# A delta-rule attention with a GELU block on one core: V of chunk 1 scaled between the query masks, exponents moved forward on ScalarE

## The chip, the cores and the metric

The kernel runs on one core of a Trainium2 chip. The metric is device time in microseconds for one execution. Four runs of the kernel before took 670.16 to 671.1 us, with a median of 670.89 us.

The engines are TensorE (PE in the profile; its weight loads are PEld), VectorE (DVE), ScalarE (ACT) and GpSimd (POOL). SyncE (SP) issues the loads. Each engine works its own instructions strictly in the order of its queue and waits on semaphores for the others.

## What is computed

The first part is a delta rule: for each of 4 x 8 heads a 48 x 48 state is carried over 768 steps. Its outputs, put side by side for the 8 heads, are 3072 rows of 384 numbers, which go through a two-layer block with an exact GELU.

```python
k_n = k / (np.linalg.norm(k, axis=-1, keepdims=True) + 1e-06)
for t in range(S):
    y[:, :, t] = einsum('bhd,bhde->bhe', q[:, :, t], state)
    v_old = einsum('bhde,bhd->bhe', state, k_n[:, :, t])
    state = state + beta_t * einsum('bhd,bhe->bhde', k_n[:, :, t], v[:, :, t] - v_old)
x = y.transpose(0, 2, 1, 3).reshape(B * S, H * D)
h = x @ w_in                      # 384 -> 2048
out = (0.5 * h * (1 + erf(h / sqrt(2)))) @ w_out
```

Shapes: q, k, v are 4 x 8 x 768 x 48, beta is 4 x 8 x 768, w_in is 384 x 2048, w_out is 2048 x 384. Both weights come in as 64-bit floats and are decoded to 32 bits on the chip.

## The kernel before

**Chunks and units.** The 768 steps are cut into 12 chunks of 64. In a chunk there are two units (`a` = 0, 1), each with two batches on the 128 partitions and all 8 heads. The recurrence inside a chunk is turned into products of K with K (`grams`), of Q with K (`queries`), an inverse of a unit lower triangular matrix by `eliminate_steps`, and per chunk: `against_state` (W from V and the state), `solve` (U = inverse times W, copied from PSUM by eight ScalarE copies, L603), `use` (P times U into PSUM, L615), `update` (the addition to the state, L624, on TensorE), `next_state` (that addition into the state, L629, on VectorE), `read` (four ScalarE copies of the outputs of a unit, L636) and `turn` (transposed outputs xT for the feed-forward part). The feed-forward part of a chunk is sixteen `fc1` groups (L677) with a Gelu each on ScalarE (L679), then the second layer (L690 in the first chunks).

Chunks 0 and 1 are the list `first`: four units, `first[:2]` of chunk 0 and `first[2:]` of chunk 1. Chunk 0 has no state before it, so its W is V times a factor (L562, GpSimd). For chunk 1, V is multiplied by the norms with `scale_v` (L332, GpSimd) before `against_state` of that chunk reads it, at 78.17 us in the profile. `masked` (L405, GpSimd) multiplies the query products P of a unit by a triangular mask, 128 x 512 each; `use` reads P, at 51.6 us for chunk 0 and at 90.2 us for chunk 1.

**Weights.** A weight group of 768 columns is decoded in four steps. `begin(n)` takes the exponent bits (VectorE, L218). `exponents(n)` shifts them (ScalarE, L223). `mantissas(n)` is two VectorE instructions (L228, L230). `signed(n)` is two more (L235, L236), reads the exponents, and asks SP to `fetch` the raw weights of four groups further on, into the same buffer. Groups 0 to 7 are w_in, 8 to 15 are w_out. The raw weights of groups 8 to 10 are fetched early, into buffers that nothing else uses then (`slots`).

**Who sets the order.** There are two parts. Up to `by_hand.close()` the order of all five queues is that of the program text: loads, transposes, `grams`, the elimination of chunk 0 and 1 (VectorE, 18 to 40 us), `back0` to `back2` (the inverse is transposed into XM and Zf; `back2` also clears parts of Zf, once on ScalarE, L464, and three times on GpSimd, L466), two levels of `join`, decoding of groups 0 to 2, and chunk 0. The second level of `join` ends in four ScalarE copies into Zf (L499). After it, VectorE's order is that of a list with due times (`plan`), written out by the program. The order of the other four queues is then set by the framework's planner from its own estimates of when things are ready.

The loads of this part stand on SP in the order of the text; q of chunk 2 and k of chunk 3 go into buffers that become free only when the query transposes have read them.

Of the kernel before, what the change touches and what calls it, by code (L numbers as in the profile page):

```python
# [16 lines left out]
def kernel(  # L17
# [35 lines left out]
    NA = B // 2  # L53
# [15 lines left out]
    def dn(name):  # L69
        return ps.tile([128, 2, 512], F32, tag="dn", name=name)  # L70
# [22 lines left out]
    def fetch_in(dst, src, u, queues=(nc.sync, nc.sync)):  # L93
        rows = slice(u.c * C, (u.c + 1) * C)
        for p in range(2):
            queues[p].dma_start(out=dst[HALF[p]],
                                in_=src[2 * u.a + p, :, rows, :].rearrange("h t d -> t h d"))

    for c in range(NC):
        for a in range(NA):  # L100
            u = tiles[c, a] = Unit()
# [37 lines left out]
    def load_v(c):  # L139
        if c >= NC:  # L140
            return
        for a in range(NA):
            u = tiles[c, a]
            u.V = io.tile([128, H, D], F32, tag="V", name="V", bufs=4)
            fetch_in(u.V, v, u)
# [4 lines left out]
    first = [tiles[c, a] for c in range(2) for a in range(NA)]  # L150
# [48 lines left out]
    def fetch(n):  # L199
        if n >= len(w_parts):  # L200
            return
        dst, src = w_parts[n]
        if n < n_in:
            raw = stage[:, n % NS * 2 * WG:(n % NS + 1) * 2 * WG]
        else:
            raw = slots[(n - n_in) % len(slots)]
        w_raw[n] = raw.rearrange("q (n w) -> q n w", w=2)
        raw = raw.rearrange("q (m n w) -> q m n w", m=dst.shape[1], w=2)
        for m in range(dst.shape[1]):
            nc.sync.dma_start(out=raw[:, m], in_=src[:, m])  # L210
# [3 lines left out]
    def begin(n):  # L214
        e = su.tile([128, WG], U32, tag="w_e", name="w_e")
        raw = w_raw.pop(n)
        halves[n] = w_parts[n][0].rearrange("q m n -> q (m n)"), raw[:, :, 0], raw[:, :, 1], e
        nc.vector.tensor_scalar(e, raw[:, :, 1], 20, 0x7FF, op0=ALU.logical_shift_right,  # L218
                                op1=ALU.bitwise_and)

    def exponents(n):
        e = halves[n][3]
        nc.scalar.activation(e, e, ACT.Relu, bias=lim[:, 0:1], scale=float(2 ** 23))  # L223

    def mantissas(n):
        dst, lo, hi, e = halves[n]
        bits = dst.bitcast(U32)
        nc.vector.tensor_scalar(bits, hi, 0xFFFFF, 0x100000, op0=ALU.bitwise_and,  # L228
                                op1=ALU.bitwise_or)
        nc.vector.scalar_tensor_tensor(dst, lo, 2.0 ** -32, bits, ALU.mult, ALU.add)  # L230

    def signed(n):

        dst, lo, hi, e = halves.pop(n)
        nc.vector.scalar_tensor_tensor(e, hi, 0x80000000, e, ALU.bitwise_and, ALU.bitwise_or)  # L235
        nc.vector.scalar_tensor_tensor(dst, dst, 2.0 ** -20, e.bitcast(F32), ALU.mult, ALU.mult)  # L236
        after = n + (NS if n < n_in else len(slots))
        if (after < n_in) == (n < n_in):
            fetch(after)
# [91 lines left out]
    def scale_v(u, engine=nc.gpsimd):  # L331
        engine.tensor_tensor(u.V, u.V, ns[u.c][:, u.a].unsqueeze(2).to_broadcast([128, H, D]),  # L332
                                op=ALU.mult)
# [70 lines left out]
    def masked(u, engine=nc.gpsimd):  # L404
        engine.tensor_tensor(u.P, u.P, mask_h, op=ALU.mult)  # L405
# [144 lines left out]
    def pairs(ap, s):  # L550

        return ap.rearrange("q (k s r) d -> q k s r d", s=2, r=2)[:, :, s]
# [3 lines left out]
    def against_state(us):  # L556

        for u in us:
            u.W = wk.tile([128, H, D], F32, tag="W", name="W")
            u.y = None  # L560
            if u.c == 0:
                nc.gpsimd.tensor_tensor(u.W, u.V,  # L562
                                        ng[:, u.a].unsqueeze(2).to_broadcast([128, H, D]),
                                        op=ALU.mult)
                continue
            u.psK = dn("psK")[:, :, 0:2 * NP * D].rearrange("q r (x j d) -> q x r j d", x=2, d=D)
            for x in range(2):
                for j in range(NP):
                    for r, p in QUADS:
                        rows = slice(r * C, r * C + D)  # L570
                        to = HALF[p ^ (j % 2)] if x and u.c > 1 else HALF[p]
                        nc.tensor.matmul(u.psK[to, x, r, j, :], lhsT=(u.Qt if x else u.Kt)[rows, p, j, :],  # L572
                                         rhs=St[rows, u.a, p, j, :], start=True, stop=True)
        for u in us:
            if u.c == 0:
                continue
            gm = gms[u.c // 2][:, u.t]
            u.y = wk.tile([128, H, D], F32, tag="y", name="y")
            nc.scalar.copy(heads(u.y), u.psK[:, 1])  # L579
            nc.vector.tensor_tensor(heads(u.W), u.psK[:, 0], heads(u.V), op=ALU.subtract)  # L580
            nc.vector.tensor_tensor(u.W, u.W, gm.unsqueeze(2).to_broadcast([128, H, D]),
                                    op=ALU.mult)

    def quarters(ap):

        return ap.rearrange("q p (k r d) -> q p k r d", r=2, d=D)

    def solve(us, copies=(nc.scalar.copy, nc.scalar.copy)):
        psU = dn("psU")
        for u in us:  # L590
            zf = Zf[(u.c // 2) % 2]
            u.psU = quarters(psU[:, :, u.a * NP * D:(u.a + 1) * NP * D])
            for k in range(NP // 2):
                for r in range(2):
                    for p, s in SIDES:
                        h = 4 * k + 2 * s + r
                        nc.tensor.matmul(u.psU[HALF[p ^ s], p, k, r, :],  # L597
                                         lhsT=zf[HALF[p], u.t * H + h, :],
                                         rhs=u.W[HALF[p], h, :], start=True, stop=True)
        for u, copy in zip(us, copies):  # L600
            u.U = wk.tile([128, H, D], F32, tag="U", name="U")
            for p, s in SIDES:
                copy(pairs(u.U[HALF[p]], s), u.psU[HALF[p ^ s], p])  # L603

    def use(us):

        for u in us:
            psY = dn("psY")
            u.psY = quarters(psY[:, :, 0:NP * D])
            u.psS = psY[:, :, NP * D:2 * NP * D].rearrange("q p (j d) -> q p j d", d=D)  # L610
            for k in range(NP // 2):
                for r in range(2):
                    for p, s in SIDES:
                        h = 4 * k + 2 * s + r
                        nc.tensor.matmul(u.psY[HALF[p ^ s], p, k, r, :], lhsT=u.P[HALF[p], h, :],  # L615
                                         rhs=u.U[HALF[p], h, :], start=True, stop=True)
            if u.c > 0:
                update(u)

    def update(u):  # L620
        if u.c < NC - 1:
            for j in range(NP):
                for r, p in QUADS:
                    nc.tensor.matmul(u.psS[HALF[r], p, j, :], lhsT=u.Kp[HALF[p], 2 * j + r, :],  # L624
                                     rhs=u.U[HALF[p], 2 * j + r, :], start=True, stop=True)
# [5 lines left out]
    def read(u, copy=nc.scalar.copy):  # L631
        u.x = wk.tile([128, H, D], F32, tag="x", name="x")
        for p, s in SIDES:
            dst, src = pairs(u.x[HALF[p]], s), u.psY[HALF[p ^ s], p]
            if u.c < 2:
                copy(dst, src)  # L636
            else:
                nc.vector.tensor_tensor(dst, src, pairs(u.y[HALF[p ^ s]], s), op=ALU.add)  # L638
# [219 lines left out]
        fetch_in(Qp[2 + a][:, :, 0:D], k, tiles[3, a])  # L858
    for n in range(2, NS):
        fetch(n)  # L860
    for n in range(n_in, n_in + len(slots)):
        fetch(n)
    load_v(1)
    third = [tiles[2, a] for a in range(NA)]
    for u in third:
        transposed(u, (0,))
# [9 lines left out]
    nc.vector.scalar_tensor_tensor(ng, gms[0][:, 0:NA], -1.0, ns[0], ALU.mult, ALU.mult)  # L876
    back0[0](*back0[1:])
    against_state(first[:NA])
    for u in first:
        masked(u)  # L880
    back1[0](*back1[1:])
    for a in range(NA):
# [1 line left out]
    back2[0](*back2[1:])  # L884
    for a in range(NA):
        join(0, (a,), 1)
    for u in first[NA:]:
        scale_v(u)
    begin(0)
    exponents(0)  # L890
    mantissas(0)
    begin(1)
    mantissas(1)
    solve(first[:NA])
    exponents(1)
    signed(0)
    use(first[:NA])
    for u in first[:NA]:
        read(u)
    signed(1)  # L900
    for u in first[:NA]:
        turn(u)
    for u in first[:NA]:
        update(u)
    begin(2)
    exponents(2)
    mantissas(2)
    signed(2)
    for u in first[:NA]:
# [103 lines left out]
```

## Time and profile before

| what | value |
|---|---|
| median of four runs | 670.89 us |
| the profiled execution: its own time | 671.1 us |
| its span, first to last instruction | 669.4 us |
| PE busy | 642.1 us (96%) |
| DVE busy | 452.6 us (68%) |
| ACT busy | 229.2 us (34%) |
| POOL busy | 82.2 us (12%) |
| PE clock granted, mean | 0.985 |

All times below are of this execution, counted from the span's start. The page gives totals by engine and a row of tenths for 40 slices of the span. Further views of the same profile are used: the waits (who waited for whom), the timeline (a row has start, duration, engine, line, operation, tiles, shapes and count, and in brackets the idle time before it with what ended it; neighbours of one kind are merged into one row), the groups of one line (shortest, median and longest duration), windows (busy time of each engine in a stretch, with the granted clock), the loads, and the chain of waits that ended last. Durations of two neighbours on an engine overlap by up to 0.1 us.

### The profile page before, as it was taken

The numbers are of one execution on the slowest core, as the hardware profiler recorded it, in microseconds if no ns is written. First come the engines' busy times: TensorE is split into PE (matmuls) and PEld (weight loads), VectorE is DVE, ScalarE is ACT, GpSimd is POOL, SyncE is SP. The second block draws the span as 40 slices with busy tenths as digits, with TensorE's granted clock in tenths as the row PEclk, the third lists the DMA queues.
The fourth block names the chain that finished last, engine by engine and source line by source line (L and its number), as shares of the span: only waits on it lengthen the run. The fifth ranks groups of instructions, "written<-read, shape, count | busy, mean of one in ns | idle before, by whom it ended". The sixth has DMA issues, their size and how long they took to land.

```text
span 669.4 us, 21705 instructions
## 1 busy us (share of the span) xinstructions
PE 642.1 (96%) x9542; PEld 560.3 (84%) x9542; DVE 452.6 (68%) x921; ACT 229.2 (34%) x605; POOL 82.2 (12%) x82
## 2 busy tenths in 40 slices
PE   6868999999999999999999999999999999999997
PEld 5656775776689989989989989989989989989997
DVE  6999999995799846489846479846479844324021
ACT  3357744714342143142143142143142133122220
POOL 4051300104010021111021110021111010000000
PEclk9976999999999999999999999999999999999999
DMA  9885555203432232511342511211301210100101
GB/s 131 178 250 172 116 170 139 48 0 68 82 49 41 47 55 41 86 26 32 55 59 38 84 27 28 52 21 32 67 3 24 56 19 3 24 2 2 24 1 25
DMA packets 158431, 39.76 MB, mean 59 GB/s; under 512 B 150016, under 2 KB 153216, under 8 KB 158336
## 3 DMA queue, kind: packets, MB, share of 16 engines
q1 hardware_dynamic: 152464, 33.40, 26.3%
q10 hardware_dynamic: 5872, 4.97, 3.2%
q8 instruction: 75, 1.23, 0.7%
q14 instruction: 20, 0.16, 0.1%
HBM read 33.62 MB, written 4.72 MB: 57 GB/s over the span
## 4 chain that ended last, share of the span: by engine, by line
PE 84%; DVE 10%; ACT 2%; issue 2%; DMA 1%; SPq 0%; DVEq 0%; ACTq 0%
PE psH L677 36%; PE psX L715 12%; PE psY L715 12%; PE psZ L715 4%; PE psO L690 4%; PE psK L572 3%; PE psJ L517 3%; PE psG L367 3%; PE psU L597 2%; PE psY L615 2%; DVE tmp L442 2%; DVE Nu L444 2%; DVE w_e L235 1%; PE psY L624 1%; DVE w_out_sb L236 1%
## 5 line engine op out<-in xcount | busy, mean ns | idle before, releaser
L677 PE MATMUL psH<-xT,w_in_sb 128*128 128x256 f32 x1152 | 262.3, 384 | 1.5 <-ACT G L679 1.4
L677 PEld LDWEIGHTS psH<-xT,w_in_sb 128*128 128x128 f32 x1152 | 216.0, 191 | 33.0 <-ACT G L679 3.0
L679 ACT ACTIVATE G<-psH 128x256 f32<-128x256 f32 x192 | 73.5, 383 | 180.6 <-PE psH L677 168.5
L442 DVE TENSOR_TENSOR tmp<-Nu 128x30 f32<-128x30 f32 (+9 forms) x180 | 62.4, 347 | 5.1
L444 DVE TENSOR_TENSOR Nu<-Nu,tmp 128x30 f32<-128x30 f32 (+9 forms) x180 | 61.2, 340 | 6.2
L715 PE MATMUL psX<-w_out_sb,G 128*128 128x192 f32 x320 | 56.2, 329 | 0.0
L715 PE MATMUL psY<-w_out_sb,G 128*128 128x192 f32 x304 | 54.2, 329 | 0.6
L715 PEld LDWEIGHTS psX<-w_out_sb,G 128*128 128x128 f32 x320 | 52.2, 190 | 0.7
L715 PEld LDWEIGHTS psY<-w_out_sb,G 128*128 128x128 f32 x304 | 49.1, 190 | 2.1 <-DVE u L761 1.8
L690 PE MATMUL psO<-w_out_sb,G 128*128 128x384 f32 x128 | 45.2, 496 | 1.6 <-DVE w_out_sb L236 1.6
L660 ACT COPY xT<-psX 128x384 f32<-128x384 f32 x24 | 11.4, 478 | 102.8 <-PE psX L659 102.7
L306 POOL TENSOR_TENSOR n<-n,half 128x16 f32<-128x16 f32 x10 | 29.4, 2938 | 86.4 <-DVE n L281 65.5
L690 PEld LDWEIGHTS psO<-w_out_sb,G 128*128 128x128 f32 x128 | 23.0, 190 | 17.1 <-DVE w_out_sb L236 4.0
L603 ACT COPY U<-psU 64x192 f32<-64x192 f32 x96 | 30.1, 314 | 20.1 <-PE psU L597 18.8
L402 DVE TENSOR_TENSOR P<-psG,mask 128x1024 f32<-128x1024 f32 x10 | 12.2, 1224 | 34.9 <-PE psG L367 34.9
L466 POOL MEMSET Zf<- 32x512 f32 x23 | 12.4, 541 | 154.9 <-DVE Zf L457 153.9
L724 DVE TENSOR_TENSOR S<-G 128x512 f32<-128x512 f32 x20 | 13.8, 688 | 25.8 <-ACT G L679 25.8
L580 DVE TENSOR_TENSOR W<-psK,V 128x384 f32<-128x384 f32 x22 | 12.1, 552 | 28.2 <-ACT y L579 28.1
L332 POOL TENSOR_TENSOR V<-V,n 128x384 f32<-128x384 f32 x18 | 17.2, 963 | 106.9 <-DMA V<-in_v_dram 56.4
L638 DVE TENSOR_TENSOR x<-psY,y 64x192 f32<-64x192 f32 x80 | 28.3, 354 | 0.9
L715 PE MATMUL psY<-T,G 128*128 128x192 f32 x160 | 28.2, 329 | 0.0
L715 PE MATMUL psX<-T,G 128*128 128x192 f32 x160 | 28.1, 329 | 0.0
(138 smaller groups left out, 868.2 us busy)
## 6 DMA issues: line engine op xcount, KB each, us to landing
Kp<-in_k_dram SPq DMA_DIRECT2D x76, 96.0 KB, 3.3
w_out_sb<-in_moe_w_in_dram SPq DMA_DIRECT2D x24, 256.0 KB, 4.4
V<-in_v_dram SPq DMA_DIRECT2D x48, 96.0 KB, 2.9
out_dram<-o_sb ACTq DMA_DIRECT2D x46, 96.0 KB, 2.2
w_raw<-in_moe_w_out_dram SPq DMA_DIRECT2D x10, 384.0 KB, 4.9
Zf<-in_moe_w_out_dram SPq DMA_DIRECT2D x6, 384.0 KB, 4.3
Qp<-in_q_dram SPq DMA_DIRECT2D x64, 32.0 KB, 2.2
Qp<-in_q_dram SPq DMA_DIRECT2D x16, 96.0 KB, 4.4
```

Of the source, the lines that this page charges most:

```text
L306: nc.gpsimd.tensor_tensor(flat, flat, half, op=ALU.pow)
L367: nc.tensor.matmul(psG[HALF[p], r, i * NP + j, :], lhsT=u.Kt[rows, p, j, :], rhs=(u.Qt if x else u.Kt)[rows, p, j, :], start=True, stop=True)
L442: nc.vector.tensor_tensor(tmp, nu[:, j + 1:, j:j + 1].to_broadcast([128, n, j]), nu[:, j:j + 1, 0:j].to_broadcast([128, n, j]), op=ALU.mult)
L444: nc.vector.tensor_tensor(nu[:, j + 1:, 0:j], nu[:, j + 1:, 0:j], tmp, op=ALU.add)
L517: nc.tensor.matmul(psJ[to, i, :], lhsT=(xm if level else off)[rows, u, :], rhs=zf[rows, u, HB:C] if level else xm[rows, u, :], start=True, ...
L572: nc.tensor.matmul(u.psK[to, x, r, j, :], lhsT=(u.Qt if x else u.Kt)[rows, p, j, :], rhs=St[rows, u.a, p, j, :], start=True, stop=True)
L603: copy(pairs(u.U[HALF[p]], s), u.psU[HALF[p ^ s], p])
L638: nc.vector.tensor_tensor(dst, src, pairs(u.y[HALF[p ^ s]], s), op=ALU.add)
L677: nc.tensor.matmul(psH, lhsT=w_in_sb[:, f // 2, m, f % 2 * 128:(f % 2 + 1) * 128], rhs=xTs[c][:, m, :], start=(m == 0), stop=(m == NM - 1))
L679: nc.scalar.activation(G[:, f, :], psH, ACT.Gelu)
L690: nc.tensor.matmul(u.psO, lhsT=G[:, f, u.a * 128:(u.a + 1) * 128], rhs=w_out_sb[:, f, :], start=(f == 0), stop=(f == NF - 1))
L715: nc.tensor.matmul(ps_, lhsT=lhs[:, f, :], rhs=rhs[:, f, :], start=first and f == 0, stop=f == FH - 1, skip_group_check=not first)
```

## The change

Three moves in the hand-ordered part; no instruction is added or taken away.

The load of V of chunk 1 stands on SP before the three early fetches of w_out instead of after them. On GpSimd the two scalings of V of chunk 1 stand between the masks of chunk 0 and those of chunk 1; they were the last thing there, after the memsets of `back2`. On ScalarE `exponents(1)` stands before the copies of `solve` instead of after them, and `exponents(2)` between the two `read`s instead of after both `turn`s; for that `begin(2)` goes forward on VectorE, from after `signed(1)` to before it.

```diff
     for n in range(2, NS):
         fetch(n)
+    load_v(1)
     for n in range(n_in, n_in + len(slots)):
         fetch(n)
-    load_v(1)
...
     against_state(first[:NA])
-    for u in first:
+    for u in first[:NA]:
+        masked(u)
+    for u in first[NA:]:
+        scale_v(u)
+    for u in first[NA:]:
         masked(u)
     back1[0](*back1[1:])
...
     for a in range(NA):
         join(0, (a,), 1)
-    for u in first[NA:]:
-        scale_v(u)
     begin(0)
     exponents(0)
     mantissas(0)
     begin(1)
     mantissas(1)
+    exponents(1)
     solve(first[:NA])
-    exponents(1)
     signed(0)
+    begin(2)
     use(first[:NA])
-    for u in first[:NA]:
-        read(u)
+    read(first[0])
+    exponents(2)
+    read(first[1])
     signed(1)
     for u in first[:NA]:
         turn(u)
     for u in first[:NA]:
         update(u)
-    begin(2)
-    exponents(2)
     mantissas(2)
     signed(2)
```

## The prediction

> **What bounds the kernel now.** The page comes first: it says which engine is full and at what clock.
>
> ```profile
> PE 642.1 (96%) x9542; PEld 560.3 (84%) x9542; DVE 452.6 (68%) x921; ACT 229.2 (34%) x605; POOL 82.2 (12%) x82
> ...
> PEclk9976999999999999999999999999999999999999
> ```
>
> TensorE is busy for 96% of the span and its idle time lies early. In a view of the span by windows it works 41.8 of the first 60 us and 56.5 of the next 60; from 200 to 600 us it is 99.7 to 99.9% busy. All the change is before 63 us, and what it moves reaches the end only through the state of things at about 117 us, where TensorE last waits for VectorE. So I read next the waits between 60 and 118 us, of PE and of DVE:
>
> ```profile
> PE psO L690 <- DVE w_out_sb L236: 1.6, 3, 0.9
> PE psH L677 <- ACT G L679: 1.4, 3, 0.6
> ```
> ```profile
> DVE w_e L235 <- ACT w_e L223: 1.4, 2, 0.9
> ```
>
> VectorE decodes weights there, 58.2 of 60 us busy, and the chain of waits runs along its decode lines until 117.4, then along TensorE. TensorE has 1.6 us of slack against that line. So one number decides: how much sooner or later the decode line leaves the hand-ordered part, which is when `begin(3)` starts, 62.60 us. The timeline of 39.5 to 72 us:
>
> ```profile
> 41.63 4.97 POOL L405 TENSOR_TENSOR P<-P,mask 128x512 f32<-128x512 f32 x4
> ...
> 47.78 2.18 POOL L466 MEMSET Zf<- 32x512 f32 x3 [1.17 <-DVE Zf L457]
> 47.96 0.96 DVE L228 TENSOR_SCALAR w_in_sb<-w_out_sb 128x768 uint32<-128x768 uint32 x1
> ...
> 50.04 2.14 POOL L332 TENSOR_TENSOR V<-V,n 128x384 f32<-128x384 f32 x2
> 50.30 1.18 DVE L228 TENSOR_SCALAR w_in_sb<-w_out_sb 128x768 uint32<-128x768 uint32 x1
> 51.25 2.64 ACT L603 COPY U<-psU 64x192 f32<-64x192 f32 x8 [0.38 <-PE psU L597]
> ...
> 51.52 1.47 DVE L230 SCALAR_TENSOR_TENSOR w_in_sb<-w_out_sb,w_in_sb 128x768 f32<-128x768 uint32 x1
> ...
> 57.22 0.55 DVE L228 TENSOR_SCALAR w_in_sb<-w_out_sb 128x768 uint32<-128x768 uint32 x1
> ...
> 57.81 0.96 DVE L230 SCALAR_TENSOR_TENSOR w_in_sb<-w_out_sb,w_in_sb 128x768 f32<-128x768 uint32 x1
> 58.23 1.96 PE L624 MATMUL psY<-U,Kp 64*64 64x48 f32 x64
> ...
> 59.68 0.96 DVE L235 SCALAR_TENSOR_TENSOR w_e<-w_out_sb,w_e 128x768 uint32<-128x768 uint32 x1 [0.91 <-ACT w_e L223]
> ...
> 61.66 1.02 DVE L629 TENSOR_TENSOR St<-St,psY 128x384 f32<-128x384 f32 x2
> 62.60 0.55 DVE L218 TENSOR_SCALAR w_e<-w_out_sb 128x768 uint32<-128x768 uint32 x1
> ```
>
> Three things to see. The decode instructions take 0.55 (L228) and 0.96 us (L230) alone, but 1.18 and 1.47 while GpSimd scales V (50.04 to 52.18), and L228 took 0.96 beside the first memset. `signed(2)` (L235 at 59.68) waited 0.91 for its exponents on ScalarE. ScalarE sat idle 0.38 before the U copies.
>
> **GpSimd.** W ends at 41.68; two masks at 1.27 each (4.97 / 4 with a little overlap) end at 44.15. The two scalings take 0.83 each by the row of the same shape that ran with no such VectorE work beside it (L562, 1.62 for two), or up to 1.14 by their own slowest row. VectorE then does transposes and reads PSUM; the masks kept 1.27 through these, so I take 0.83: end 45.8. The other masks end at 48.2 (48.9 at most), the first at 46.95. The memsets, now at 47.78, follow: the first ends at 49.05 by my value, 49.7 at worst. `solve` needs the first memset and the second of the Zf copies on ScalarE (48.40 + 2 x 0.37 = 49.14; it began at 49.23). So no delay, at worst 0.5.
>
> **VectorE against GpSimd.** Today the overlaps cost 0.96-0.55, 1.18-0.55 and 1.47-0.96: 0.41 + 0.63 + 0.51 = 1.55 us. The last two go, 1.14. But the fourth mask now runs from 46.95 to 48.2, over `begin(0)` (issued 47.50, 0.54 today). 1.18 fits an instruction that waits until the first scaling ends (51.07) and then takes 0.4. By that row `begin(0)` ends at 48.6, 0.55 late; the bounds are 0 and 0.63. The memset beside `mantissas(0)` keeps its 0.41. Net gain 1.14 - 0.55 = 0.59: `signed(0)` starts at 52.32, not 52.91, and `begin(1)` ends at 50.93, not 50.38.
>
> The Trainium skill, "SBUF — State Buffer", section "Who interferes with whom", states this lock and speaks against the change: a VectorE instruction in a two-port mode, or with two SBUF inputs against a GpSimd one that reads SBUF, fully blocks until the other ends. It fits the rows, L230 under a memset included (48.96, 0.96: no delay). Without this lock at `begin(0)` the net would be 1.14.
>
> **ScalarE, and TensorE behind it.** `exponents(1)` (0.94) now stands before the eight U copies. It waits for `begin(1)`, 50.93, ends at 51.89, and the copies start at 51.91, not 51.25: 0.66 late (part of the 0.94 falls into the 0.38 in which ScalarE was idle). Queued behind it are the U copies, and TensorE's `use` waits for them. The x copies of the first unit are not late (54.76 today, with the exponents ahead of them; 54.57 then). `exponents(2)`, 0.94, then stands before the second unit's x copies; its `begin(2)` is done by 54.8 and x is read until 55.9, so it waits for nothing. Everything after is 0.66 late: both xT copies, the second `turn`, and `update` on TensorE, 58.89 to 60.85, not 58.23 to 60.19. The first fc1 group starts at 60.78, not 60.12. That is the price of the change.
>
> **The decode line.** Spacing from start to start by the rows: `signed` 1.97 (the second time 1.87), `begin` 0.47, `mantissas` 1.46. `signed(0)` 52.32, `begin(2)` 54.29, `signed(1)` 54.76, `mantissas(2)` 56.63, `signed(2)` 58.09 (its exponents are done at 56.8: the 0.91 wait is gone), ready for `next_state` at 60.06. Now TensorE is late: the first state can be added at 60.06, the second waits for `update`, 60.85 + 0.1. `begin(3)` starts at 61.42. Against 62.60 the decode line is 1.18 us ahead. Freeing `begin(0)` of its block would bring only 0.12 more, since `exponents(1)` would still wait for `exponents(0)` to end at 50.87.
>
> **From there to 117 us.** ScalarE waited 2.87 us for `begin(3)` before 63.19; its row of exponents, squares and Gelu, which paces TensorE from 65 to 73, comes 1.18 sooner. TensorE: first group 60.78 to 63.5 (half clock until 63.4, six matmuls of 0.48), join to 64.8, second group to 66.3 (65.81 today), third at 66.3 (66.39 today), fourth at 69.0 (69.56), sixth at 71.75 (72.93). The late start is absorbed in TensorE's waits for Gelu, and TensorE is also 1.1 ahead. Even if it were not, the 1.6 us of slack would cover it.
>
> The clock: it was half from 42.9 to 63.4 (0.50 in the windows view). The 3.41 us before its return were fully busy (3.41 of 3.41), the 3.41 before those, without a return, 3.00. By my times TensorE works without a gap from 58.06, so that window stays full. The skill's "TensorE: Matmul & The Clock Gate", Part 1, has the same rule, a busy window of some 3.4 us on a free-running grid, so the place of the grid may differ between executions.
>
> **The V load.** Its four issues move from 39.06 to 34.25, the six weight issues go back by 2.7 us. From issue to landing V took 7.6 us in today's backlog; the median of such loads up to 160 us is 4.0. That gives 40.9 to 44.5 for the last, needed at 44.15 and 45.0; fewer bytes are ahead, so I take 42, no cost (0.4 at worst). The weights that go back are first read at 85.49: nothing. No SP wait is passed, and SP next issues at 53.88.
>
> **The sum.** Span 669.4 - 1.18 = 668.2; the profiled execution took 671.1, 1.7 around its span, so 669.9. The median is 0.2 below that: 670.89 - 1.2 = 669.7.
>
> **Rivals.** *The weights cap it.* `begin(7)` started at 77.58; its three loads were issued at 71.73 to 73.3 and take 4.4 to land, so about 77.5: no slack. The SP queue up to them is a string that starts with the load after `signed(2)`, 60.67, then 59.0. If its string shrinks less than its start, the gain at 77.6 is 0 to 0.6: 670.3 to 670.9.
>
> *Slower: the planner sorts ScalarE anew.* After the hand-ordered part only VectorE's order is fixed. A Gelu waits for its matmuls. `exponents(3)` must end before `signed(3)`, 65.00 today; it has 0.88 to spare, so from a start after 64.07 the decode line is later than today. With one Gelu ahead (first group ends at 63.5, then 0.2 and 0.36) it starts at 64.1: gain gone. With two (66.3) it starts at 66.9, ends at 67.8: 2.8 late, 673.7. For it: the planner's times of the prologue have changed. Against: the same instructions in the same program order.
>
> *The planner sorts better:* TensorE idles 3.5 us between 60 and 120, so at most 3.5 sooner, likely 1.5 to 2.5: 668.4 to 669.4.
>
> **Numbers.** A difference under 0.2%, 1.34 us, is about what a measurement of this kernel can tell from no change: 669.55 to 672.23 counts as same. Forecast 0.53 (gain 0.9 to 1.6 with the spread of such medians, 669.3 to 670.0; 0.28 of it beyond 0.2%); cap 0.08; slower by sorting, or by a lost clock window, 0.29 (one part in thirty of it small enough for same); better 0.10. Faster 0.38, same 0.34, slower 0.28. The range 668.8 to 672.8 leaves out part of the two sortings, not more than 0.2.
>
> **What would show it.** Right: L228 and L230 of group 1 at 0.55 and 0.96; `begin(0)` near 1.1; U copies at 51.9; no wait before `signed(2)`; `begin(3)` near 61.4; 1.6 us of psO waits for L236 left, all 1.2 earlier. Wrong: a wait of GpSimd for V, `solve` after 49.4, half clock beyond 63.4, or ScalarE's order changed between 60 and 73.

## The result and the profile after

The changed kernel takes 671.85 us (median of 32 runs, 670.64 to 673.28) against 670.75 us for the kernel before (52 runs, 669.81 to 672.25). The ratio is 1.0016, with a 95% interval of 1.0011 to 1.0021: it is 1.1 us slower, and the forecast was 1.2 us faster. The profiled execution took 671.49 us with a span of 669.7.

Two lines of the page, the busy time of the engines and the granted clock in 40 slices, look nearly as before:

```profile
PE 642.1 (96%) x9542; PEld 560.4 (84%) x9542; DVE 451.8 (67%) x921; ACT 229.1 (34%) x605; POOL 82.2 (12%) x82
...
PEclk9566999999999999999999999999999999999999
```

VectorE has 0.8 us less of busy time, most of it the contention with GpSimd that the change takes away. The clock is low in one more slice of the first 60 us, which delays nothing up to `begin(3)` (below), and it is back at 62.5 us, sooner than the 63.4 of before.

One thing has to be set right before times are compared. The first 15 us, where the first loads are waited for, do not take the same time in every execution (L434 on VectorE starts at 14.62 before and at 14.33 after), so everything after them is shifted. The last transposition of `back2` on VectorE (L457), which stands ahead of all that the change touches there, starts at 45.72 us before and at 45.43 us after. I take such a shift out (here 0.29) where I write "aligned".

The timeline of the changed kernel, 40 to 63 us (start, duration, engine, line, operation, tiles, shapes, count, and in brackets the idle time before with what ended it):

```profile
43.81 1.62 POOL L332 TENSOR_TENSOR V<-V,n 128x384 f32<-128x384 f32 x2
...
47.22 1.08 DVE L218 TENSOR_SCALAR w_e<-w_out_sb 128x768 uint32<-128x768 uint32 x1
...
50.56 0.55 DVE L228 TENSOR_SCALAR w_in_sb<-w_out_sb 128x768 uint32<-128x768 uint32 x1
...
51.15 0.96 DVE L230 SCALAR_TENSOR_TENSOR w_in_sb<-w_out_sb,w_in_sb 128x768 f32<-128x768 uint32 x1
51.70 2.64 ACT L603 COPY U<-psU 64x192 f32<-64x192 f32 x8
...
57.80 0.95 DVE L235 SCALAR_TENSOR_TENSOR w_e<-w_out_sb,w_e 128x768 uint32<-128x768 uint32 x1
...
58.68 1.96 PE L624 MATMUL psY<-U,Kp 64*64 64x48 f32 x64
...
60.77 0.55 DVE L629 TENSOR_TENSOR St<-St,psY 128x384 f32<-128x384 f32 x1 [0.37 <-PE psY L624]
...
61.25 0.55 DVE L218 TENSOR_SCALAR w_e<-w_out_sb 128x768 uint32<-128x768 uint32 x1
```

All of the hand-ordered part went as forecast. `begin(0)`, the row at 47.22, takes 1.08; L228 and L230 of group 1 are back at 0.55 and 0.96; `signed(2)` at 57.80 has no idle time before it; `next_state` waits 0.37 for `update`; and `begin(3)` starts at 61.25, 1.35 sooner by the clock of the trace and 1.06 aligned.

The lead is still 0.91 aligned at `signed(7)`, and it is gone one weight group later. The waits between 60 and 120 us, of VectorE and of TensorE:

```profile
DVE w_e L235 <- ACT w_e L223: 2.3, 1, 2.3
```
```profile
PE psO L690 <- DVE w_out_sb L236: 3.4, 4, 1.2
```

One wait of 2.3 us of a `signed` for its exponents stands where there were two of together 1.4, and TensorE's waits for decoded weights have more than doubled. The rows around this one wait, first of the kernel before (ScalarE, then VectorE):

```profile
87.48 0.94 ACT L223 ACTIVATE w_e<-w_e,lim 128x768 uint32<-128x768 uint32 x1
88.97 0.38 ACT L679 ACTIVATE G<-psH 128x256 f32<-128x256 f32 x1 [0.55 <-PE psH L677]
...
88.45 0.96 DVE L235 SCALAR_TENSOR_TENSOR w_e<-Zf,w_e 128x768 uint32<-128x768 uint32 x1 [0.47 <-ACT w_e L223]
```

and of the changed kernel:

```profile
87.86 0.38 ACT L679 ACTIVATE G<-psH 128x256 f32<-128x256 f32 x1 [1.38 <-PE psH L677]
88.14 0.93 ACT L223 ACTIVATE w_e<-w_e,lim 128x768 uint32<-128x768 uint32 x1
89.10 0.96 DVE L235 SCALAR_TENSOR_TENSOR w_e<-Zf,w_e 128x768 uint32<-128x768 uint32 x1 [2.34 <-ACT w_e L223]
```

Before, `exponents(8)` (L223) stands ahead of the third Gelu (L679) after the U copies of chunk 1, which is that of fc1 group 13. In the changed kernel it stands behind it. That Gelu waits 1.38 us for TensorE's fc1 products, and `exponents(8)`, whose input was ready (`begin(8)` started at 84.28 and takes 0.55), waits with it, and so does the whole decode line. The change does not touch this place. It lies in the part that the framework's planner orders; there the first 66 ScalarE and 299 TensorE instructions after the hand-ordered part hold all that is ordered differently. On TensorE the U products of chunk 1 are now split by fc1 products, and the products with P and K alternate in pieces.

### The profile page after: what moved, and what is told of

Same layout as the page of the kernel before. It is cut to its first block, busy times and chain, and to the rows that moved or that the text cites. A ratio compares the mean times of both kernels' runs of the same rounds, so it can differ in the third digit from the quotient of the medians.

```text
span 669.7 us, 21708 instructions
## 1 busy us (share of the span) xinstructions
PE 642.1 (96%) x9542; PEld 560.4 (84%) x9542; DVE 451.8 (67%) x921; ACT 229.1 (34%) x605; POOL 82.2 (12%) x82
## 4 chain that ended last, share of the span: by engine, by line
PE 86%; DVE 8%; ACT 2%; issue 2%; DMA 2%; SPq 0%; DVEq 0%; ACTq 0%
PE psH L677 38%; PE psX L715 12%; PE psY L715 12%; PE psZ L715 4%; PE psO L690 4%; PE psK L572 3%; PE psJ L517 3%; PE psG L367 3%; PE psU L597 2%; PE psY L615 2%; DVE Nu L444 2%; DVE tmp L442 2%; PE psY L624 1%; PE psX L659 1%; DVE w_e L235 1%
## 5 line engine op out<-in xcount | busy, mean ns | idle before, releaser
L679 ACT ACTIVATE G<-psH 128x256 f32<-128x256 f32 x192 | 73.5, 384 | 181.8 <-PE psH L677 169.8
L690 PE MATMUL psO<-w_out_sb,G 128*128 128x384 f32 x128 | 45.4, 496 | 3.5 <-DVE w_out_sb L236 3.4
L690 PEld LDWEIGHTS psO<-w_out_sb,G 128*128 128x128 f32 x128 | 23.0, 190 | 19.3 <-DVE w_out_sb L236 6.6
```

The costliest lines, as they stand in the source:

```text
L679: nc.scalar.activation(G[:, f, :], psH, ACT.Gelu)
L690: nc.tensor.matmul(u.psO, lhsT=G[:, f, u.a * 128:(u.a + 1) * 128], rhs=w_out_sb[:, f, :], start=(f == 0), stop=(f == NF - 1))
```

## The experiments

Theory A: the hand-ordered part gains what was forecast, and the planner's new order takes more than that back, at `exponents(8)`. Rivals: the gain was not real (bought by a delay of TensorE that comes due later), or VectorE's lead is worth nothing at the end. "Held" below means that the order of ScalarE and TensorE after the hand-ordered part is written out, by dependences between neighbours of a queue that fix their order and add no wait. The order of SP and GpSimd there is the same in all kernels.

The main reading is one table. The offsets are against the profiled execution of the kernel before, aligned; negative is sooner. L236 of group 15 is the last decode step, at 117.4 us before. The median differences are against the kernel before in the same series of runs (that of the changed kernel is the result above); the three series, e1 to e4, e5 with p1 to p3, and q1 to q4, are each from one chip.

| kernel | order after the hand part | `begin(3)` | `signed(8)` | L236 of group 15 ends | last VectorE instruction | median, us | ratio, 95% interval |
|---|---|---|---|---|---|---|---|
| changed kernel | new | -1.06 | +0.94 | +1.19 | +0.60 | +1.10 | 1.0016 [1.0011, 1.0021] |
| e1 changed | held to old | -1.08 | -1.10 | -1.11 | -1.39 | -0.97 | 0.9986 [0.9978, 0.9995] |
| e2 before | held to new | -0.03 | +0.96 | +0.97 | +0.72 | +1.00 | 1.0016 [1.0007, 1.0024] |
| e3 changed | new but for one swap | -1.11 | -0.17 | -0.17 | +0.08 | -0.28 | 0.9993 [0.9984, 1.0001] |
| e4 changed | tied to the U copies | -1.06 | +0.95 | +0.93 | +0.42 | +1.17 | 1.0019 [1.0010, 1.0027] |
| p1 V part only | held to old | +0.02 | +0.03 | +0.06 | +0.11 | +0.21 | 1.0000 [0.9992, 1.0009] |
| q1 V part only | planner's: new | 0.00 | +1.02 | +1.01 | +0.62 | +1.15 | 1.0016 [1.0007, 1.0024] |
| p2 exponents part only | held to old | -1.02 | -0.78 | -0.78 | -1.08 | -0.80 | 0.9987 [0.9978, 0.9996] |
| q2 changed, GpSimd's move undone | planner's: old | -1.01 | -1.00 | -0.98 | -1.26 | -0.94 | 0.9986 [0.9977, 0.9995] |
| q3 as e1 | held to old | -1.05 | -1.04 | -1.02 | +0.50 | -0.76 | 0.9991 [0.9983, 1.0000] |
| e5 as e1, `exponents(8)` first | held | -0.99 | -1.52 | -1.49 | -1.11 | -1.66 | 0.9978 [0.9970, 0.9987] |
| q4 as e5 | held | -1.05 | -1.58 | -1.59 | -1.97 | -1.91 | 0.9971 [0.9961, 0.9982] |
| p3 V scaled early, loaded late | held to old | +4.99 | +5.00 | +5.03 | +5.16 | +4.66 | 1.0074 [1.0061, 1.0086] |

### Moves and order, each alone

e1 is the changed kernel with the old order; e2 is the kernel before with the new order.

```diff
         emit(*plan)
+    issue_in_order(tc, nc, here, mybir.EngineType.Activation, ...)   # the first 82
+    issue_in_order(tc, nc, here, mybir.EngineType.PE, ...)           # the first 299
```

> The changed kernel, with the queues of ScalarE and TensorE after the hand-ordered part pinned to the places they have in the kernel before (82 ScalarE and 299 TensorE instructions; SP and GpSimd are the same in both already). Theory A, the planner's new order is the loss: the decode line leaves the hand-ordered part at 61.25 as in the changed kernel and keeps its lead of 1.0 to 1.2 us to 117 us; signed(8) waits about 0.5 for exponents(8), not 2.34; the time is 0.7 to 1.2 us under the kernel before. Rival B, the loss is in the moves themselves (GpSimd beside begin(0), U copies late, clock): still about 1.1 us over the kernel before.

> The kernel before, with the queues of ScalarE and TensorE after the hand-ordered part pinned to the places they have in the changed kernel. Theory A: the Gelu of group 13 stands ahead of exponents(8), so signed(8) waits 1.5 to 2.5 us and the time is 1 to 2 us over the kernel before, with none of the three moves made. Rival B: within 0.3 us of the kernel before.

`signed(8)` on VectorE, first in e1, then in e2:

```profile
87.09 0.96 DVE L235 SCALAR_TENSOR_TENSOR w_e<-Zf,w_e 128x768 uint32<-128x768 uint32 x1 [0.55 <-ACT w_e L223]
```
```profile
88.74 0.96 DVE L235 SCALAR_TENSOR_TENSOR w_e<-Zf,w_e 128x768 uint32<-128x768 uint32 x1 [1.37 <-ACT w_e L223]
```

e1 came out 0.97 us under the kernel before and e2 1.00 over it. So the moves are worth what theory A says, and the new order costs the same by itself, though e2's wait of 1.37 us is under the 1.5 to 2.5 that was expected. The table says why the two do not simply add up, -1 and +1, in the changed kernel: with the new order `signed(8)` comes 0.94 to 1.02 late whether the decode line arrives 1.06 early (changed kernel) or on time (e2, q1). Where `exponents(8)` stands behind a Gelu, TensorE's fc1 products set its time, and a lead of VectorE is just a longer wait: 2.34 us in the changed kernel, 1.37 in e2.

### One swap

e3 leaves the planner's new order and only puts `exponents(8)` ahead of the Gelu of group 13; e4 ties it directly to the end of the U copies and ahead of the Gelu of group 11, and leaves the rest to the planner.

```diff
# e3
+    issue_in_order(tc, nc, here, mybir.EngineType.Activation, [[32, 1], [59, 1]])
# e4
+    issue_in_order(tc, nc, here, mybir.EngineType.Activation, [[48, 1], [32, 1], [52, 1]])
```

> The changed kernel with two neighbours on ScalarE swapped, exponents(8) ahead of the Gelu of group 13; every other queue as in the changed kernel. Theory A: exponents(8) starts at 86.4, not 88.14, signed(8) near 87.3, not 89.10, and the decode line at 117 is 1.5 to 1.8 us sooner than in the changed kernel; time 1.2 to 1.8 us under the changed kernel, 0.2 to 0.7 under the kernel before. Rival B: as the changed kernel, within 0.3 us. Rival C, the new TensorE order costs too: gains 0.5 to 1 us on the changed kernel and stays over the kernel before.

> The changed kernel with exponents(8) on ScalarE directly behind the U copies of chunk 1, ahead of the Gelus of groups 11, 12 and 13. Theory A: no wait at signed(8); the decode line keeps its lead of 1.2 and gains the 0.47 that the kernel before waits there; TensorE waits up to 0.9 more for the Gelu of group 11 but has slack; time 1.2 to 1.7 us under the kernel before. Rival: TensorE's wait at group 13 is not made good, time equal to the kernel before.

The swap takes the decode line from 1.19 late to 0.17 ahead, 1.36 us (1.5 to 1.8 was expected) of the 2.30 that lie between the changed kernel and e1, so this one place carries most of the loss. It does not bring back all. `signed(8)` still waits 1.17: in the new TensorE order, with fc1 products between those of U, ScalarE waits 1.50 for the first U copy of chunk 1 (0.72 in e1), and `exponents(8)` comes after these copies. No run holds the order of TensorE alone, so this rest is read from one trace. The median, 0.28 under the kernel before, has an interval that reaches just over no change, so e3 by itself does not show a gain.

e4 missed its aim. The planner answered by putting two other Gelus ahead of `exponents(8)`, one of which waited 1.65 us; `signed(8)` waited 2.50, and the time was that of the changed kernel. It is no test of "behind the U copies", but another case of the same thing: an exponents step behind a waiting Gelu costs what that Gelu waits.

### The two parts of the change, and who turned the order

p1 is the kernel before with only the V part, order held; q1 is the same with nothing held. p2 is the kernel before with only the exponents part, order held. q2 is the changed kernel with only this undone, and nothing held:

```diff
-    for u in first[:NA]:
-        masked(u)
-    for u in first[NA:]:
-        scale_v(u)
-    for u in first[NA:]:
+    for u in first:
         masked(u)
...
         join(0, (a,), 1)
+    for u in first[NA:]:
+        scale_v(u)
     begin(0)
```

> The kernel before with only the V part of the change (load_v(1) before the early fetches, scalings between the masks); ScalarE's exponents and begin(2) where they were, later orders as before. Theory A (V takes GpSimd out of VectorE's way, but signed(2) still waits for exponents(2), which stands behind the second xT copy on ScalarE, 58.71): begin(0) grows to about 1.1, L228 and L230 of group 1 fall to 0.55 and 0.96, signed(0) starts 0.5 to 0.6 sooner, and the wait of signed(2) grows from 0.91 by as much: begin(3) stays at 62.5 to 62.7 and the median within 0.2 of the kernel before. Rival B (the contention with GpSimd is what the decode line pays): begin(3) 0.5 to 0.6 sooner and the median 0.4 to 0.6 lower.

> The kernel before with only the V part of the change, and nothing held: the planner orders ScalarE and TensorE itself, and the order it then writes after the hand-ordered part is that of the changed kernel (Gelu of group 13 ahead of exponents(8)). Theory A (moving V on GpSimd saves nothing by itself, as p1 showed, and costs the new order): signed(8) waits 1.2 to 2.4 us for ScalarE, the decode line is about 1.0 later at 117 us, and the median is 0.7 to 1.3 above the kernel before, ratio 1.0010 to 1.0020. Rival B (the new order hurts only a line that has been made earlier): within 0.3 of the kernel before.

> The kernel before with only the exponents part (exponents(1), exponents(2) and begin(2) moved); V is loaded and scaled where it was, later orders as before. Theory A: L228 and L230 of group 1 stay near 1.2 and 1.5, signed(0) starts at about 52.9, but signed(2) no longer waits: it starts near 58.5, its product ends at 60.6, just when update ends, and begin(3) starts at 61.4 to 61.8, 0.8 to 1.2 sooner than before; the median is 0.6 to 1.0 under the kernel before, within 0.35 of e1. Rival B (both parts are needed, since each saves its own wait): begin(3) gains less than 0.6 and the median less than 0.5.

> The changed kernel with one thing undone: the two scalings of V stand on GpSimd after the memsets again (the load of V stays early). Nothing is held; the planner's order after the hand-ordered part is then that of the kernel before. Theory A (the exponents part brings nearly all, and it is GpSimd's move that changes the order): L228 and L230 of group 1 are back at about 1.2 and 1.5, begin(3) is still 0.9 to 1.1 ahead, signed(8) waits 0.3 to 0.7 as in p2, and the median is 0.6 to 1.1 under the kernel before, ratio 0.9984 to 0.9991. Rival B (without the move the contention on VectorE takes the gain): ratio 0.9993 or more.

The times of all four are those of theory A. The V part alone frees VectorE of the contention and gains nothing. In p1 `signed(0)` starts 0.57 sooner aligned, but `signed(2)` waits as long as before for ScalarE, while `signed(1)` waits 0.61 besides:

```profile
59.19 0.96 DVE L235 SCALAR_TENSOR_TENSOR w_e<-w_out_sb,w_e 128x768 uint32<-128x768 uint32 x1 [0.92 <-ACT w_e L223]
```

(VectorE in p1; the trace starts 0.51 sooner than that of the kernel before.) The wait of `signed(2)` did not grow as the expectation had it; the 0.59 was taken at `signed(1)`, one group earlier. With nothing held, in q1, the V part costs 1.15 us, with ScalarE's rows in the order of the changed kernel:

```profile
88.04 0.38 ACT L679 ACTIVATE G<-psH 128x256 f32<-128x256 f32 x1 [1.38 <-PE psH L677]
88.32 0.93 ACT L223 ACTIVATE w_e<-w_e,lim 128x768 uint32<-128x768 uint32 x1
```

The exponents part alone brings nearly all the gain. p2 and q2 keep the slow L228 and L230 of group 1, 1.19 and 1.47 us, and still have `begin(3)` 1.01 to 1.02 sooner, against 1.05 to 1.08 with both parts (e1, q3). In q2 the planner writes the old order by itself, and `signed(8)` waits little:

```profile
87.18 0.96 DVE L235 SCALAR_TENSOR_TENSOR w_e<-Zf,w_e 128x768 uint32<-128x768 uint32 x1 [0.37 <-ACT w_e L223]
```

q2 differs from the changed kernel in nothing but the place of the two scalings. So it is this move of two GpSimd instructions, within a V part that gains nothing by itself, that turned the order of ScalarE and TensorE behind the hand-ordered part; it costs the most 40 us later, at `exponents(8)`. Why the planner's estimates answer to it I did not follow.

p2 also hints at what the early load of V does for other transfers. In p2, with V loaded late, `begin(7)` waited for a load:

```profile
76.84 0.56 DVE L218 TENSOR_SCALAR w_e<-w_out_sb 128x768 uint32<-128x768 uint32 x1 [0.81 <-DMA Qp<-in_k_dram]
```

Its lead fell from 1.01 to 0.22 at that row. It was back at 0.78 by `signed(8)`, because that no longer had to wait for ScalarE. In q2, with V loaded early, `begin(7)` was 0.90 ahead. This is one trace of each.

### The load of V

p3 scales V between the masks as the changed kernel does, but loads it where the kernel before does.

```diff
-    for u in first:
+    for u in first[:NA]:
+        masked(u)
+    for u in first[NA:]:
+        scale_v(u)
+    for u in first[NA:]:
         masked(u)
...
         join(0, (a,), 1)
-    for u in first[NA:]:
-        scale_v(u)
     begin(0)
```

> The kernel before with the scalings of V between the masks but V loaded where it was, after the early fetches; exponents where they were, later orders as before. V landed at 46.8 to 48.6 in the kernel before, so GpSimd should wait for it from 44.2, end the scalings at about 49.5, the masks at about 52 and the first memset at about 53. Theory A (the load is what lets the scalings move): solve and the U copies start 3.5 to 4.5 late (near 55.2), update ends near 64, VectorE waits about 2 us for it before begin(3), which starts at 64.5 to 65.5, and the median rises by 1.5 to 3.5. Rival B (the lead of TensorE over the decode line at 117 us, 1.6, and the room of the later waits absorb it): begin(3) is late but the median rises by less than 0.7.

GpSimd waited for the load, and the U copies with it (GpSimd, ScalarE and VectorE rows of p3):

```profile
48.07 1.93 POOL L332 TENSOR_TENSOR V<-V,n 128x384 f32<-128x384 f32 x2 [3.73 <-DMA V<-in_v_dram]
...
56.41 2.65 ACT L603 COPY U<-psU 64x192 f32<-64x192 f32 x8 [5.38 <-PE psU L597]
...
60.05 0.96 DVE L235 SCALAR_TENSOR_TENSOR w_e<-w_out_sb,w_e 128x768 uint32<-128x768 uint32 x1 [3.31 <-ACT w_e L223]
```

The direction is that of theory A, the size is not: 4.66 us, where 1.5 to 3.5 was expected. I had left out that the masks behind the scalings then run beside VectorE's decoding and slow each other (the two masks 3.51 us for 2.50, `begin(1)` 1.62 for 0.55), and that `exponents(1)` stands behind the U copies, so `signed(1)` waits 3.31 for it. A `begin(3)` that is 4.99 us late is 5.16 late at the last VectorE instruction: nothing of it is absorbed.

### A better order

e5 is e1 with one step moved in the held order of ScalarE: `exponents(8)` directly behind the U copies, ahead of the Gelus of groups 11 and 12. q4 repeats e5 beside q3, which repeats e1.

```diff
-    ..., [41, 8], [52, 1], [55, 1], [32, 1], [59, 1], ...
+    ..., [41, 8], [32, 1], [52, 1], [55, 1], [59, 1], ...
```

> The changed hand-ordered part; after it the order of ScalarE and TensorE is that of the kernel before, but for one step: exponents(8) stands directly behind the U copies, ahead of the Gelus of groups 11 and 12. Theory A (what a Gelu ahead of exponents(8) costs is what signed(8) waits): the wait of signed(8) for ScalarE, 0.55 us in e1, is gone, the decode line is 0.4 to 0.55 further ahead from there to 117 us, and the median is 0.3 to 0.55 below that of e1, 669.1 to 669.4. Rival B (by then TensorE, or the landing of the weights, sets the pace): the wait goes and reappears on the decode line at the next begin or signed that waits for a DMA, or two Gelus later as a TensorE wait, and the median stays within 0.15 of e1's 669.65.

> e1 once more, beside q2 and q4 on one chip, since single medians of two calls differ by some tenths. Theory A (with the exponents moved, taking the scalings out of VectorE's way adds only what is left after the wait for update): within 0.25 of q2, ratio 0.9982 to 0.9990. Rival B (the contention's 0.59 is worth its size): 0.4 to 0.6 under q2.

> e5 once more beside q3. In the trace of e5 the decode line was 1.5 ahead at 117 us and not 1.1 as in e1, but TensorE waited 1.2 us for a Gelu that stood behind exponents(8), and its end was 1.1 ahead of before, not 1.4 as in e1. Theory A (what counts is the decode line): 0.3 to 0.5 under q3. Rival B (the Gelu that is put back costs TensorE as much as the decode line gains): within 0.2 of q3, either sign.

The wait of `signed(8)` is gone in both, and the decode line is 0.4 to 0.6 further ahead. ScalarE and VectorE of q4:

```profile
85.34 0.94 ACT L223 ACTIVATE w_e<-w_e,lim 128x768 uint32<-128x768 uint32 x1
...
86.31 0.96 DVE L235 SCALAR_TENSOR_TENSOR w_e<-Zf,w_e 128x768 uint32<-128x768 uint32 x1
```

TensorE pays with a wait of 1.2 us for the Gelu behind it, where it waited 0.3 in e1 and q3. A part comes back out of its waits for decoded weights: 1.1 us in e5 and q4 for 1.6 in e1 and q3. Medians: q4 668.91 against 670.06 for q3 in the same series, 1.15 less; e5 against e1, each by its own difference to the kernel before, 0.69 less. Theory A had 0.3 to 0.55, which both exceed, so its direction holds and the size stays uncertain. At 0.9971 and 0.9978 of the kernel before, this is faster than both kernels.

q3 came out at 0.9991, just outside the 0.9982 to 0.9990 that was expected, and 0.18 us above q2, within the 0.25. That q3 is no faster than q2 speaks against rival B. The intervals of the two ratios are too wide to decide it, but the offsets are not: at `begin(3)` and at 117 us q3 is 0.04 sooner than q2, not 0.4 to 0.6. Once the exponents have moved, the contention's 0.59 is worth nothing that the runs can tell.

## Why the prediction was wrong

**Right, to 0.12 us: everything up to `begin(3)`.** In aligned times, forecast first: U copies 51.91 and 51.99; `signed(0)` 52.32 and 52.31; `update` 58.89 and 58.97; first fc1 60.78 and 60.86; `begin(3)` 61.42 and 61.54. The masks of chunk 0 ended at 44.15, as forecast, and the scalings ran without waiting for V. `begin(0)` took 0.54 more (0.55 forecast): it was issued at 47.22, the fourth mask ended at 47.89, and it ended 0.41 after that. The Trainium skill, "SBUF — State Buffer", section "Who interferes with whom", has this as a lock that the later instruction waits for, and the row agrees to 0.14 us: a full 0.55 behind the mask would have been that much later.

**Right where the order is kept: the sum.** Forecast were 1.18 us; e1 gave 0.97 and q3 0.76 by medians, and the decode line is 1.02 to 1.11 ahead at 117 us in both. With the order kept, the step from `begin(3)` to the end holds, and so does the claim that TensorE's later start (0.66 us forecast, 0.74 measured) is absorbed.

**The step that failed: "From there to 117 us".** It took the order of ScalarE and TensorE after the hand-ordered part as given. It was not, and the decode line was 1.19 late there instead of 1.18 ahead, aligned. The rival "the planner sorts ScalarE anew" named the mechanism, a Gelu ahead of exponents. It priced it only at `exponents(3)`, where the decode line leaves the hand-ordered part, and not along the rest of it. One of its signs of being wrong did show, ScalarE's order between 60 and 73 us: the first Gelu, at 63.11, stands ahead of `exponents(4)`, at 64.07; before, `exponents(4)` at 65.16 stands ahead of the first Gelu at 65.98. There it cost nothing, since no `signed` before `signed(8)` waits. At `exponents(8)` there was no slack at all: `signed(8)` already waited 0.47 for it, and the next Gelu in the queue waited 0.55 for TensorE. The price could have been read from the two rows of the kernel before. A swap puts `exponents(8)` 0.28 after the start of that Gelu, at 89.25 instead of 87.48, 1.77 late, less what TensorE gains by its own new order. That Gelu started 0.82 sooner, aligned (87.86 and 88.97), and 1.77 - 0.82 = 0.95 is what the table has.

**The reason against that rival was wrong too.** "The same instructions in the same program order" does not keep the planner's order: q2 differs from the changed kernel in GpSimd's move alone and gets the old order.

**Not worked out: what each part is worth.** The text states a net gain of 0.59 us for the V part, but that is a gain at `signed(0)`. Its own last step takes `begin(3)` from `update`, "Now TensorE is late", and not from `signed(0)`. With its own spacings the exponents alone start `signed(0)` at 52.91 and the two additions of `next_state` at 60.65; with 0.94 for these, as in the kernel before, `begin(3)` starts at 61.59. That is 1.01 of the 1.18; p2 has it at 61.58 aligned. So by its own numbers the V part was worth 0.17, and the runs show 0.03 to 0.07 beside the new exponents (e1 and q3 against p2 and q2) and 0 beside the old ones (p1), where `signed(1)` and `signed(2)` wait for ScalarE all the same. A gain that runs into a wait a few rows further on should have been struck from the account: the exponents alone were the change's worth, 1.0 us.

**The cap by the weights** did show, not in the changed kernel (0.2 us before a `begin`) but in p2, 0.81 us at the very `begin(7)` that the rival named. (The profile puts this wait down to a load of K; what `begin(7)` reads is raw weights.)

## What to carry to other kernels

Where a planner orders part of the queues, an edit has two effects, what it does and what the planner then does elsewhere; compare the order of each queue in the two kernels before reading times, and hold the order when the edit itself is to be judged. Where one line of work decides the time, look at each step that another engine does for it, and at what stands ahead of that step in the other engine's queue: a step that is ready, but stands behind an instruction that waits for the busiest engine, starts only after that wait, however early the line arrives. Try the parts of a change one by one, since the one that gains nothing can be the one that costs.

## What the runs showed that I had not expected

Two executions of one program can differ by 2 us behind the part that an experiment changes, most of it through TensorE's clock. e1 and q3 are the same kernel; the profiled execution of q3, 671.56 us, is the slowest of its twelve (669.26 to 671.56). Its decode line is as far ahead at 117 us as that of e1, and the loss lies between 152 and 158 us: q3's matmuls are 0.05 us later than those of e1 at 152 us, aligned with each other, and 2.19 later at 158. TensorE first idled 0.69 us before L367, for nothing that the profile shows (0.17 in e1), and then the same four products of L690 took 2.84 us, for 1.56 in e1:

```profile
155.22 1.56 PE L690 MATMUL psO<-w_out_sb,G 128*128 128x384 f32 x4
```
```profile
156.02 2.84 PE L690 MATMUL psO<-w_out_sb,G 128*128 128x384 f32 x4
```

A view of q3 by windows of 1 us (busy time of TensorE, granted clock, share of the DMA engines, GB/s) has the clock at half there, with TensorE busy all the time:

```profile
157.00:158.00 1.00, 1.00 (x2) 0.50 0.61 114
```

Worked out from such windows (0.57 in the one before, 0.50 in the one after, 0.72 in the fourth), the clock was at half for 0.86 + 1 + 1 + 0.56 = 3.4 us. The Trainium skill, "TensorE: Matmul & The Clock Gate", Part 1, has the clock fall after a window of about 3.4 us in which TensorE is idle. That does not fit these rows: TensorE was busy for 7.72 of the 9 us from 145 to 154 us, and no idle time in them was over 0.7. In e3 the idle time at the same place was 0.80, TensorE was busy for 8.57 of the 10 us from 145 to 155 us (8.72 in q3), and the clock stayed full, so neither the length of this idle time nor the busy share over these 10 us decides it. What does is open. It means that a single profile of this kernel does not tell a difference of 1 us at the end; the offsets at 117 us and the medians do.
